# Moving tiles of the pairs made two words longer and read from the third word on, in a float32r attention and squared-ReLU kernel

## The chip, the cores and the metric

One core of one Trainium2 chip runs the whole program in one launch. The metric is the device time of a run in microseconds (us). The kernel before was run three times: the median is 1607.09 us, the lowest 1606.95, the highest 1607.5.

## What is computed

Two stages. First, attention through 32 inducing points: the points attend to the 12480 tokens of each of 4 batches, then every token attends to the 32 results. Second, a wide layer with a squared ReLU, on all 49920 tokens. Cut to what matters:

```python
def mab(q, kv):
    s = scale * (q @ kv.transpose(0, 2, 1))
    s = s - s.max(-1, keepdims=True)
    a = np.exp(s)
    a /= a.sum(-1, keepdims=True) + 1e-09
    return a @ kv
h = mab(I, x)              # I: (4, 32, 128), x: (4, 12480, 128)
y = mab(x, h)              # (4, 12480, 128)
...
h = y @ w_in               # (49920, 128) @ (128, 2048)
r = np.maximum(h, 0.0)
g = s * (r * r) + b
out = g @ w_out            # (49920, 2048) @ (2048, 128)
```

## The kernel before

The tokens are cut into 104 blocks of 480 (26 for each batch). The attention weights of a block on the 32 points stand in a tile `a2t` of 128 x 480 words: 32 rows of rounded values (float32r) and 32 rows of what the rounding left, each twice. The 32 results times `w_in` are formed once for each batch and stand in `wst` (128 x 2048, float32r), in parts that match the rows of `a2t`. So one matmul with `wst` as weights (stationary) and `a2t` as the streamed operand (moving) gives 128 of the 2048 hidden values of 480 tokens. Sixteen such matmuls make a block; the function `pair` issues them two at a time (L834), 8 pairs for each block.

What follows a pair: a ReLU of the two results (`r`, L849 on ACT or L851 on DVE), a product ReLU(h)·r, which is the square in float32 (`g`, L870 on DVE), a square rounded to float32r (`g1`, L911 on ACT, for one pair or for two at a time), and the difference of the two, `g2` = `g` − `g1` (L888, on POOL for most pairs, on DVE for the rest). Then the second layer: `out_part` (L936) multiplies `g1` with `w_hi` and with `w_lo`, the rounded and the left-over part of `w_out`, and `g2` with `w_hi`: three matmuls of 128 x 128 weights and 480 moving columns for each 128 hidden values, all accumulated in one PSUM bank. So a pair needs 2 matmuls of L834 and 6 of L936, all float32r. Only the first five pairs are done another way (`NATIVE = 5`): their squares in plain float32 times `w_out` in float32. At the end of a block the sum is scaled (L944) and stored (L948). Between the pairs stand the attention of later blocks (`attend`) and the first attention of the next batch (`scores`, `top`, `values`, `points`).

The order of all this is set when the program is built, by a small planner (`Plan`): each piece of work names its engine, an assumed time and what it waits for, and the planner picks. It knows nothing of addresses.

`a2t` comes in a ring of 3 buffers, `g2` in 8, `g1` in 4 (of four 480-word rows each, for two pairs), `g` in 4, `r` in 2. Except for the first block, an `a2t` tile is filled by four DMAs from the tile `hl` (`spread`, L805, on SP's queue). In the first block it is made by four transposes with a float32r identity `identr` (L788, in `attend_first`) and a copy. `identr` is written once at the start (L216) and is used nowhere else. `accb` is a tile of the same size in the pool `sm`: the sums of `values`, used from the second batch's preparation on (L670, L672, L692).

In the built program each tile begins at a multiple of 32 bytes of its partition. The moving tiles `a2t`, `g1` and `g2`, and with them every 480-word row of them, begin at multiples of 64 bytes. Of the three `a2t` buffers one begins at a multiple of 256 bytes, the two others 128 bytes behind one; the rows of `g1` and `g2` begin 64 or 192 bytes behind one. The last tile of the memory ends 64 bytes below the end of the partition's 224 KiB.

Of the kernel before, what the change touches and what calls it, by code (L numbers as in the profile page):

```python
# [11 lines left out]
F32R = mybir.dt.float32r  # L12
# [7 lines left out]
P = 128  # L20
T = 120
NQ = 4
BLK = T * NQ
# [124 lines left out]
def tile_attn_relu2(ctx: ExitStack, tc: tile.TileContext, xT, xN, indT, w_in, w_out, s_rep, b_rep, outT):  # L148
# [12 lines left out]
    const = ctx.enter_context(tc.tile_pool(name="const", bufs=1))  # L161
# [3 lines left out]
    p2 = ctx.enter_context(tc.tile_pool(name="p2", bufs=2))  # L165
    wst_pool = ctx.enter_context(tc.tile_pool(name="wst", bufs=2))
    sm = ctx.enter_context(tc.tile_pool(name="sm", bufs=2))
    ew = ctx.enter_context(tc.tile_pool(name="ew", bufs=1))
# [29 lines left out]
    def ring_in_order(name, bufs):  # L198

        n, free = ring(name, bufs)  # L200
        if n == 0:
            plan.events[name, "got", -1] = 0.0
        return n, (free, (name, "got", n - 1))
# [8 lines left out]
    bias = const.tile([P, 1], F32, name="bias")  # L212
    ident = const.tile([P, P], F32, name="ident")
    make_identity(nc, ident)
    identr = const.tile([P, P], F32R, name="identr")
    nc.vector.tensor_copy(out=identr, in_=ident)  # L216
    ones = const.tile([P, M], F32, name="ones")
    nc.vector.memset(ones, 1.0)
# [21 lines left out]
    def landing(us):  # L240

        dma[0] = max(dma[0], plan.end + 3.0) + us
        return dma[0]
# [458 lines left out]
    a2t, halves = {}, {}  # L702

    def attend(b, g, ps, *waits):
# [42 lines left out]
        for q in mine:  # L747
            plan.spawn(spread(b, g, q), SPREAD, plan.end + LAT)

    def attend_first(ps):  # L750
# [36 lines left out]
            w = A[:, q].rearrange("p r s i -> p (r s i)")  # L787
            nc.tensor.transpose(ps[:, q * T:(q + 1) * T].bitcast(F32R), w, identr[0:T, 0:T])  # L788
        yield dict(ACT=0.57, DVE=0.66), 0.0, *free
        t = p2.tile([P, BLK], F32R, name="a2t", bufs=3)  # L790
        plan.set(("a2t", "got", n))
        copy(t, ps[:, 0:BLK])
        a2t[0, 0] = t, n
# [3 lines left out]
    def spread(b, g, q):  # L797

        turn, free = ring_in_order("a2t", 3)
        yield "SP", 2.4, *free, ("hl", b, g)  # L800
        t = p2.tile([P, BLK], F32R, name="a2t", bufs=3)
        plan.set(("a2t", "got", turn))
        hl, n, left = halves[b, g]
        for r in range(P // M):
            nc.sync.dma_start(  # L805
                out=t[M * r:M * (r + 1)].bitcast(F32), in_=hl[M * q:M * (q + 1), r % 2].bitcast(F32)
            )
        left.remove(q)
        if not left:
            plan.set(("hl", n))  # L810
        a2t[b, GR * g + q] = t, turn
        plan.events["a2t", b, GR * g + q] = landing(0.7)
# [10 lines left out]
    def pair(k):  # L823
# [18 lines left out]
        q = quad[k - n]  # L842
# [40 lines left out]
        n2, free2 = ring("g2", 8)  # L883
        yield ("Pool", 2.237, ("Q", k), free2) if kind == "P" else ("DVE", 1.065, C_U, ("Q", k), free2)
        hi = q["g1_t"][:, half, :]
        g2 = ew.tile([P, 2, BLK], F32R, name="g2", bufs=8)
        eng = nc.gpsimd if kind == "P" else nc.vector
        eng.tensor_tensor(out=g2, in0=g, in1=hi.bitcast(F32), op=ALU.subtract)  # L888
        plan.set(("h", turn) if kind == "D" else ("g", g_turn))
# [9 lines left out]
    def square(k0):  # L899

        q = quad[k0]
        yield "ACT", 0.893, *([] if "g1_t" in q else [q["g1"][1]])
        done = [n for n, us in q["R"] if us + LAT <= plan.start + 0.01]
        lo, hi = done[0], done[-1] + 1
        del q["R"][:len(done)]
        if hi - lo == 2:
            plan.extend(0.8)
        if "g1_t" not in q:
            q["g1_t"] = ew.tile([P, 4, BLK], F32R, name="g1", bufs=4)
        sl = slice(2 * lo, 2 * hi)  # L910
        nc.scalar.activation(out=q["g1_t"][:, sl, :], in_=q["r_t"][:, sl, :], func=AF.Square)  # L911
        for i in range(lo, hi):
            plan.set(("Q", k0 + i))
            pr = (k0 + i) % NPAIR
            ops = [(w[:, 2 * pr + u, :], q["g1_t"][:, 2 * i + u, :]) for u in range(2) for w in (w_lo, w_hi)]
            plan.spawn(
                out_part(k0 + i, ops, 4 * MM, "w_split", lambda: g1_used(q)), k0 + i + OUT_HI, plan.end + LAT
            )
        if q["R"]:
            plan.spawn(square(k0), k0 + 1 + SQ, q["R"][0][1] + LAT)  # L920
        q["r_uses"] -= hi - lo
        if q["r_uses"] == 0:
            plan.set(("r", q["r"][0]))
# [191 lines left out]
```

## Time and profile before

| | |
|---|---|
| median of 3 runs | 1607.09 us (1606.95 to 1607.5) |
| the profiled execution: first to last instruction | 1605.5 us |
| granted TensorE clock, mean | 0.998 |
| matmul records | 8183 |
| of these float32r, 480 columns: L834 and L936 with w_hi, w_lo | 1664 + 3308 + 1654 = 6626 |
| DMA moved | 130.19 MB, mean 81 GB/s |

The page gives the profiled execution's span; of its own time around the span it shows nothing. PE, PEld, DVE, ACT, POOL and SP are the engines. [...] In grouped rows stand the count behind an x, the busy time, and the mean of one in ns; in rows in order of time the start, the length from the first start to the last end in us, and the count.

### The profile page before, as it was taken

The page shows a single profiled execution, that of the slowest core. Times are in us where ns is not written, and L with a number is a line of the kernel's source. Part 1 is how long each engine was busy: PE and PEld are TensorE (multiplying, and loading weights), DVE is VectorE, ACT ScalarE, POOL GpSimd, SP SyncE. Part 2 cuts the span into 40 slices and gives each one's busy share as a digit, 9 for nine tenths or more (in the row PEclk, how much of TensorE's full clock was granted, in tenths as well). Part 3 has the DMA queues.
Part 4 walks back from the last instruction along what each step waited for, and adds up shares of the span by engine and source line. Part 5 has one row for each costly group of instructions (what it writes and reads, how often), then busy time and mean ns, then how long its engine had stood idle before and what let it go on. Part 6 is the DMA issues. An engine that isn't in the chain of part 4 may idle for free.

```text
span 1605.5 us, 24656 instructions
## 1 busy us (share of the span) xinstructions
PE 1590.8 (99%) x8183; PEld 1294.8 (81%) x8183; DVE 1493.6 (93%) x1610; ACT 1476.7 (92%) x1694; POOL 1499.9 (93%) x677
## 2 busy tenths in 40 slices
PE   9899999999999999999999999999999999999998
PEld 6577888888887788888788787888888888888887
DVE  5999999999999999999999899999899999999997
ACT  7799989999999999999999998999999999999997
POOL 0299999999999999999999999999999999999998
PEclk9999999999999999999999999999999999999999
DMA  7332224212133233221213322321222112112100
GB/s 266 100 106 94 79 87 148 62 50 88 42 101 118 76 116 116 73 71 56 79 59 99 100 85 99 117 81 62 72 64 65 37 50 68 32 50 68 56 29 22
DMA packets 53981, 130.19 MB, mean 81 GB/s; under 512 B 11488, under 2 KB 37984, under 8 KB 53856
## 3 DMA queue, kind: packets, MB, share of 16 engines
q1 hardware_dynamic: 53856, 128.63, 25.0%
q8 instruction: 66, 1.08, 0.3%
q14 instruction: 59, 0.48, 0.1%
HBM read 73.52 MB, written 25.56 MB: 62 GB/s over the span
## 4 chain that ended last, share of the span: by engine, by line
PE 97%; DVE 1%; DMA 0%; ACT 0%; issue 0%; SPq 0%; ACTq 0%
PE x L936 67%; PE h L834 24%; PE x L712 2%; PE x L660 1%; PE x L615 1%; PE h L409 1%; DMA xt<-in_xT_dram 0%; PE x L463 0%; DVE g L870 0%; PE h L463 0%; PE x L565 0%; PE x L434 0%; PE h L434 0%; DVE wst L313 0%; DVE g L308 0%
## 5 line engine op out<-in xcount | busy, mean ns | idle before, releaser
L888 POOL TENSOR_TENSOR g<-g,g 128x960 fp32r<-128x960 f32 x670 | 1498.8, 2287 | 98.9 <-DVE g L870 79.6
L936 PE MATMUL x<-g,w_hi 128*128 128x480 f32 x3308 | 1074.3, 380 | 0.0
L911 ACT ACTIVATE g<-r 128x960 fp32r<-128x960 f32 (+1 forms) x761 | 803.2, 1079 | 34.0 <-DVE r L851 13.4
L870 DVE SCALAR_TENSOR_TENSOR g<-h,r 128x960 f32<-128x960 f32 x675 | 761.4, 1147 | 29.9 <-ACT r L849 20.5
L936 PEld LDWEIGHTS x<-g,w_hi 128*128 128x128 f32 x3308 | 621.1, 188 | 101.5 <-issue 3.1
L849 ACT ACTIVATE r<-h 128x960 f32<-128x960 f32 x638 | 612.1, 969 | 59.7 <-PE h L834 48.4
L936 PE MATMUL x<-g,w_lo 128*128 128x480 f32 x1654 | 628.7, 380 | 0.0
L834 PE MATMUL h<-a2t,wst 128*128 128x480 f32 x1664 | 511.7, 389 | 6.3 <-DVE g L870 4.6
L834 PEld LDWEIGHTS h<-a2t,wst 128*128 128x128 f32 x1664 | 300.0, 188 | 107.8 <-issue 38.8
L936 PEld LDWEIGHTS x<-g,w_lo 128*128 128x128 f32 x1654 | 310.3, 188 | 52.9 <-issue 3.1
L851 DVE TENSOR_SCALAR r<-h 128x960 f32<-128x960 f32 x194 | 223.7, 1153 | 25.3 <-PE h L834 18.8
L870 DVE SCALAR_TENSOR_TENSOR h<-h,r 128x960 f32<-128x960 f32 x157 | 181.5, 1157 | 7.9 <-ACT r L849 7.3
L888 DVE TENSOR_TENSOR g<-h,g 128x960 fp32r<-128x960 f32 x157 | 180.2, 1149 | 5.6 <-ACT g L911 0.8
L944 ACT ACTIVATE ob<-x,bias,s_sb 128x480 f32<-128x480 f32 x104 | 78.2, 752 | 14.3 <-PE x L936 14.0
L712 PE MATMUL x<-xt,hT 128*32 128x480 f32 x208 | 28.3, 578 | 0.0
L743 DVE TENSOR_TENSOR hl<-x,hl 128x480 fp32r<-128x480 f32 (+1 forms) x28 | 18.4, 656 | 10.1 <-ACT hl L179 10.1
L615 PE MATMUL x<-xt,ind_sb 128*32 128x480 f32 x156 | 21.2, 578 | 0.0
L718 DVE STREAM_TRANSPOSE x<-x 128x480 f32<-128x480 f32 (+1 forms) x28 | 19.2, 687 | 1.6 <-PE x L712 1.6
L660 PEld LDWEIGHTS x<-xn,eT 128*32 128x32 f32 (+1 forms) x630 | 17.5, 109 | 4.0 <-issue 2.7
L660 PE MATMUL x<-xn,eT 128*32 128x128 f32 (+1 forms) x630 | 20.7, 274 | 0.0
L736 DVE STREAM_TRANSPOSE x<-x 128x480 f32<-128x480 f32 (+1 forms) x28 | 19.5, 697 | 1.0
L734 DVE TENSOR_TENSOR x<-x,l 128x480 f32<-128x480 f32 (+1 forms) x28 | 18.6, 665 | 1.0
(147 smaller groups left out, 367.0 us busy)
## 6 DMA issues: line engine op xcount, KB each, us to landing
xt<-in_xT_dram SPq DMA_DIRECT2D x41, 960.0 KB, 5.3
out_dram<-ob SPq DMA_DIRECT2D x104, 240.0 KB, 2.0
a2t<-hl SPq DMA_DIRECT2D x412, 60.0 KB, 2.0
xn<-in_xN_dram SPq DMA_DIRECT2D x18, 512.0 KB, 5.1
xn<-in_xN_dram SPq DMA_DIRECT2D x18, 448.0 KB, 5.7
xt<-in_xT_dram SPq DMA_DIRECT2D x13, 480.0 KB, 4.2
wst<-hl SPq DMA_DIRECT2D x64, 64.0 KB, 2.0
r<-in_xT_dram SPq DMA_DIRECT2D x7, 480.0 KB, 9.5
```

Of the source, the lines that this page charges most:

```text
L615: nc.tensor.matmul(ps[M * q:M * (q + 1), 0:BLK], ind_sb, xt[:, q], start=True, stop=True)
L660: nc.tensor.matmul(ps[M * c:M * (c + 1), 0:P], eT[0:rows, n], xn_tiles[b, g, half][0][0:rows, n - half * TH], start=m < P // M, stop=m + P ...
L712: nc.tensor.matmul(ps[M * q:M * (q + 1), 0:BLK], hT[:, 0:M], xt[:, q], start=True, stop=True)
L736: nc.vector.transpose(out=s, in_=s)
L834: nc.tensor.matmul(h[:, u, 0:BLK], wst[:, c * P:(c + 1) * P], A, start=True, stop=True)
L849: nc.scalar.activation(out=r, in_=hv, func=AF.Relu)
L851: nc.vector.tensor_scalar(out=r, in0=hv, scalar1=0.0, scalar2=None, op0=ALU.max)
L870: nc.vector.scalar_tensor_tensor(out=g, in0=hv, scalar=0.0, in1=r, op0=ALU.max, op1=ALU.mult)
L888: eng.tensor_tensor(out=g2, in0=g, in1=hi.bitcast(F32), op=ALU.subtract)
L911: nc.scalar.activation(out=q["g1_t"][:, sl, :], in_=q["r_t"][:, sl, :], func=AF.Square)
L936: nc.tensor.matmul(o, w, g, start=first and n == 0, stop=left == 0 and n == len(ops) - 1)
L944: nc.scalar.activation(out=ob, in_=o, func=AF.Identity, bias=bias, scale=s_sb)
```

## The change

The tiles `a2t`, `g1` and `g2` get two words (8 bytes) more in each partition, and the program uses them from the third word on: the copy, the DMAs, the squares and the differences write there, and the matmuls read there. Nothing else of their shape changes. `identr` gives up its own tile and becomes the first user of the tile `accb`, which exists anyway (`bufs=1`).

```diff
-    identr = const.tile([P, P], F32R, name="identr")
+    identr = sm.tile([P, P], F32R, name="accb", bufs=1)
     nc.vector.tensor_copy(out=identr, in_=ident)
...
-        t = p2.tile([P, BLK], F32R, name="a2t", bufs=3)
+        t = p2.tile([P, BLK + 2], F32R, name="a2t", bufs=3)[:, 2:]
...
-        g2 = ew.tile([P, 2, BLK], F32R, name="g2", bufs=8)
+        g2 = ew.tile([P, 2 * BLK + 2], F32R, name="g2", bufs=8)[:, 2:].rearrange("p (u t) -> p u t", u=2)
...
-            q["g1_t"] = ew.tile([P, 4, BLK], F32R, name="g1", bufs=4)
+            q["g1_t"] = ew.tile([P, 4 * BLK + 2], F32R, name="g1", bufs=4)[:, 2:].rearrange("p (u t) -> p u t", u=4)
```

(The line of `a2t` stands twice, in `attend_first` and in `spread`.) In the built program a tile of 1928 bytes takes 1952, one of 3848 takes 3872 and one of 7688 takes 7712, so every moving row now begins 8 bytes behind a multiple of 32 bytes, and the buffers of one ring no longer stand alike against multiples of 64, 128 or 256 bytes. All tiles behind `ident` move: by 512 bytes down, and from the first `a2t` on by less. `wst`, the weights of L834, began at a multiple of 64 bytes and now begins 32 behind one; `w_hi` and `w_lo` stay where they were.

No instruction is added, removed or moved on any engine, and no wait. All that the order of PE shows is the new name of the identity in the four transposes of the first block (`x` is the PSUM tile that they write, `h` and `g` with L1052 are matmuls whose results nobody reads):

```order
 L1052 MATMUL h<-g_113 128x448 x4
 L1052 MATMUL h<-g_113 128x384
-L788 MATMUL x_85<-identr,hl 128x120 x4
+L788 MATMUL x_85<-accb,hl 128x120 x4
 L1052 MATMUL h<-g_113 128x384 x2
 L712 MATMUL x_86<-xt,hT 32x480 x4
```

The same four instructions stand at the same place. On DVE the cast that writes the identity (L216) has the new name, too; ACT, POOL and SP are the same row for row.

More of the change, by code (lines that the diff above doesn't have):

```diff
@@ L800, in spread @@
         yield "SP", 2.4, *free, ("hl", b, g)
-        t = p2.tile([P, BLK], F32R, name="a2t", bufs=3)
+        t = p2.tile([P, BLK + 2], F32R, name="a2t", bufs=3)[:, 2:]
         plan.set(("a2t", "got", turn))
```

## The prediction

> **What bounds the kernel now.** I read the page from the top: busy shares, the chain that ended last, then the stages.
>
> ```profile
> span 1605.5 us, 24656 instructions
> PE 1590.8 (99%) x8183; PEld 1294.8 (81%) x8183; DVE 1493.6 (93%) x1610; ACT 1476.7 (92%) x1694; POOL 1499.9 (93%) x677
> PE 97%; DVE 1%; DMA 0%; ACT 0%; issue 0%; SPq 0%; ACTq 0%
> PE x L936 67%; PE h L834 24%; PE x L712 2%; PE x L660 1%; PE x L615 1%; PE h L409 1%; DMA xt<-in_xT_dram 0%; PE x L463 0%; DVE g L870 0%; PE h L463 0%; PE x L565 0%; PE x L434 0%; PE h L434 0%; DVE wst L313 0%; DVE g L308 0%
> ```
>
> The chain is PE for 97% of the span, and 91% are the two lines whose moving tiles the change touches. So a nanosecond more or less in each of these matmuls is on the path from the first to the last. How many there are, and what the others cost, the groups say:
>
> ```profile
> L888 POOL TENSOR_TENSOR g<-g,g 128x960 fp32r<-128x960 f32 x670 | 1498.8, 2287 | 98.9 <-DVE g L870 79.6
> L936 PE MATMUL x<-g,w_hi 128*128 128x480 f32 x3308 | 1074.3, 380 | 0.0
> L911 ACT ACTIVATE g<-r 128x960 fp32r<-128x960 f32 (+1 forms) x761 | 803.2, 1079 | 34.0 <-DVE r L851 13.4
> L936 PE MATMUL x<-g,w_lo 128*128 128x480 f32 x1654 | 628.7, 380 | 0.0
> L834 PE MATMUL h<-a2t,wst 128*128 128x480 f32 x1664 | 511.7, 389 | 6.3 <-DVE g L870 4.6
> ```
>
> 3308 + 1654 + 1664 = 6626 float32r matmuls of 480 columns. One of them on average 1 ns faster or slower is 6.6 us, 0.41% of the span.
>
> The busy time by stages (first the stretch and its length, then PE, PEld, DVE, ACT, POOL with counts, clock, DMA share, GB/s):
>
> ```profile
> 105.00:400.00 295.00, 294.92 (x1553) 240.12 (x1552) 277.01 (x290) 272.23 (x313) 289.19 (x130) 1.00 0.28 90
> 400.00:700.00 300.00, 300.00 (x1556) 244.75 (x1555) 282.13 (x301) 279.35 (x317) 293.87 (x132) 1.00 0.27 89
> 700.00:1000.00 300.00, 299.94 (x1430) 242.96 (x1429) 281.84 (x294) 278.06 (x310) 295.38 (x133) 1.00 0.27 84
> 1000.00:1300.00 300.00, 299.82 (x1561) 248.96 (x1561) 281.55 (x299) 282.72 (x329) 293.43 (x133) 1.00 0.23 72
> 1300.00:1560.00 260.00, 260.00 (x1199) 217.15 (x1198) 249.26 (x253) 248.21 (x273) 253.71 (x114) 1.00 0.15 46
> ```
>
> PE has no idle time in these 1455 us, but POOL has little: 289.19 + 293.87 + 295.38 + 293.43 + 253.71 = 1425.6 busy, 29.4 idle. DVE has 83 us, ACT 94. The order and the share of each engine stay as they are, so however fast PE gets, POOL lets this part shrink by 29 us at most. That caps any gain: 1605.5 − 29.4 = 1576.
>
> **What one of these matmuls costs, and whether the place of its moving tile matters.** Lines of one window (duration min/median/max, first and last start), a row in order of time of the plain float32 matmuls at the start, and a piece of the chain:
>
> ```profile
> L936 PE MATMUL x<-g,w_hi x56: 373/381/385, 72.1 to 99.8; 128*128 128x480 f32 x56
> L936 PE MATMUL x<-g,wst x16: 564/566/566, 62.2 to 69.5; 128*128 128x480 f32 x16
> 64.20 1.77 PE L936 MATMUL x<-g,wst 128*128 128x480 f32 x4
> 1593.47 7.83 PE x L936 x36
> ```
>
> The pace of float32r is 7.83/36 = 217.5 ns for 480 columns. Plain float32 takes two records for one product; four of them span 1.77 us, less the last one's 0.566 that is 1.204/3 = 401 ns each, and all 16 lie within 2 ns. If float32r streamed at exactly twice that pace it would need 201 ns. It needs 16 to 17 ns more, and its records scatter over 12 ns (373 to 385) where the slow ones don't. So something in the fast stream stumbles, for some 17 ns × 6626 = 110 us in all, and not always alike.
>
> The Trainium skill, "TensorE: Matmul & The Clock Gate", section "Single matmul latency", gives (398 + N)/2.4 ns for a warm matmul: 366 for 480 columns, and 566 for 960, as two cycles for each column would be. The slow rows agree with it to the nanosecond, the float32r median of 381 is 15 above it; by the page, too, there would be some 100 us to gain.
>
> Does the place of the tile count? The three `a2t` buffers take turns, block after block, and stand differently against 256 bytes. Three blocks in turn (the middle one has the buffer at a multiple of 256), and two stretches of four matmuls each:
>
> ```profile
> L834 PE MATMUL h<-a2t,wst x16: 379/382/383, 1321.1 to 1335.3; 128*128 128x480 f32 x16
> ...
> L834 PE MATMUL h<-a2t,wst x16: 375/377/456, 1337.7 to 1348.9; 128*128 128x480 f32 x16
> ...
> L834 PE MATMUL h<-a2t,wst x16: 374/382/455, 1350.9 to 1363.0; 128*128 128x480 f32 x16
> ...
> 1334.16 0.60 PE L834 MATMUL h<-a2t,wst 128*128 128x480 f32 x2
> 1334.60 0.60 PE L936 MATMUL x<-g,w_hi 128*128 128x480 f32 x2
> 1335.04 0.60 PE L834 MATMUL h<-a2t,wst 128*128 128x480 f32 x2
> ...
> 1344.78 0.59 PE L834 MATMUL h<-a2t,wst 128*128 128x480 f32 x2
> 1345.20 0.59 PE L936 MATMUL x<-g,w_hi 128*128 128x480 f32 x2
> 1345.63 0.59 PE L834 MATMUL h<-a2t,wst 128*128 128x480 f32 x2
> ```
>
> In the first and third block the median is 382, in the middle one 377. Four matmuls in a row, two of each line, take 1335.04 − 1334.16 = 0.88 us in the first and 1345.63 − 1344.78 = 0.85 in the middle block: 220 and 212.5 ns each (to about 2.5, as the starts are rounded to 10 ns). The kinds of instructions are the same, the start of `a2t` is another. So the start does matter, by some 7 ns at this place. What no row shows is a start that is not a multiple of 64 bytes.
>
> **The change part by part.**
>
> *The matmuls (6626).* Instructions, columns and order stay. The price is the shift of the start, and rows of this trace bound it from both sides. Best: all go like the middle block, 212.5 for 217.5, −5 ns × 6626 = −33 us, of which POOL lets through 29. Worst of what the rows show: all like the first block, 220, +2.5 ns × 6626 = +17 us. I take −2 ns, −13 us: less than half of the best case, because only the ends of a stream of 480 words see the shift, and because some of what PE gains will be spent on waiting for POOL, whose steady idle share is 2%. It leans to the faster side since the stream has 17 ns to lose against 2.5 to the slow row, not since any row shows this start.
>
> *The weights.* `wst` now starts 32 bytes behind a multiple of 64. Its loads (188 ns, below) lie under matmuls that start 217 ns apart, so 30 ns more would stay hidden; beyond that each ns costs 1.7 us.
>
> ```profile
> L834 PEld LDWEIGHTS h<-a2t,wst 128*128 128x128 f32 x1664 | 300.0, 188 | 107.8 <-issue 38.8
> ```
>
> *POOL, DVE and ACT on shifted tiles.* They read and write the same 960 words from another start. I take nothing. If the shift cost POOL one more access in 240, that is 2287/240 = 9.5 ns × 670 = 6.4 us, within its 29 us. It sets the end only from 29.4 us/670 = 44 ns (1.9%) for each operation. ACT and DVE have more cover.
>
> *The a2t DMAs.* 412 of 60 KB, now landing 8 bytes off:
>
> ```profile
> L805 SPq DMA_DIRECT2D a2t<-hl x412: 507/582/2295, 57.8 to 1564.8; - x138
>   DMA wst<-hl: 1.4, 1
> DMA to landing us min/median/max: 1.9/2.0/5.5
> ```
>
> They land in 2.0 us; the only DMA that matmuls of L834 ever waited for is that of `wst`, once, 1.4 us. The ring of three tiles lets them run a block ahead (1605.5/104 = 15.4 us), so even a doubling is hidden. Without that cover it would be 2 us × 103 blocks.
>
> *The identity.* Written once, read by four matmuls until 47 us; `accb` is first written at 241.0:
>
> ```profile
> L788 PE MATMUL x<-identr,hl x4: 245/249/278, 46.5 to 46.8; 120*128 120x120 f32 x4
> L670 DVE COPY accb<-x x3: 292/292/293, 241.0 to 1020.1; 128x128 f32<-128x128 f32 x3
> ```
>
> 194 us lie between, so sharing costs no wait.
>
> Sum: 1605.5 − 13 = 1592.5 for the profiled execution. The median of the runs is 1.6 us above its span, carried over: 1594.
>
> **The rivals.**
>
> *Nothing happens.* The stumbling belongs to the fast stream itself, or to steps of 64 bytes and more; the old starts (0, 64, 128, 192 against 256) are then merely replaced by a spread that averages the same. For it: the fast and the slow `a2t` blocks already mix in the 217.5, and the new starts are spread over all places. Against it: the mean would have to stay within 0.5 ns, where places differ by 7. Time 1607.
>
> The Trainium skill, "SBUF — State Buffer", section "Specifications (TRN2)", gives 16-byte cachelines and asks for two hits in each for full bandwidth. By that rule, a start at the third word still finds two words in the first line and in the last, so it costs nothing and brings nothing. The trace agrees only in part: with four words in each line, the stream is 17 ns short of double pace already.
>
> *Slower: one more group for each stream.* If the words are fetched in groups of at least four, a start in the middle of one cuts the first and the last: 121 groups instead of 120. The stream is at its limit (it already runs below double pace), so nothing hides it: 217.5/120 = 1.8 ns × 6626 = +12 us, from the first block on, 1619. With groups of 16 words it would be 31 for 30, 7.2 ns, 48 us, 1655. It decides as soon as the fetch, not the array, sets the pace, which the 16 ns speak for. Against it: the half groups of one stream's end and the next one's start may be fetched side by side, and the blocks whose `a2t` starts 128 bytes on show that a stream can be slower with no group cut.
>
> *Faster than forecast.* If the shift removes the stumbling altogether, PE needs 201 instead of 217 and POOL sets the end: 1578.
>
> **How the numbers follow.** Faster 0.43: 1594 as the likeliest, 1577 to 1603 as its range. Nothing 0.25: 1604 to 1610. Slower 0.32: of it 0.22 around 1619 (to 1624, the row at 220 for all), 0.10 beyond, towards 1655. The range from 1577 to 1624 leaves out these 0.10 and some 0.05 below. 0.2%, 3.2 us, is about what a measurement of this kernel can tell from no change; it is 0.5 ns for each matmul.
>
> **What would show it.** In the profile of the changed kernel: a chain piece of 36 matmuls of L936 at 7.76 us or less (7.83 now) says faster, 7.89 or more the extra group. The float32r records' minimum, median and maximum (373/381/385) should move down and draw together if the stumbling goes. POOL's idle time in the five stretches should fall from 29 to about 16 us at 1594, and PE should begin to show idle time. POOL's mean should stay at 2287 ns and the DMAs of `a2t` at 2.0 us. I am wrong if PE's pace doesn't move, if it moves up, or if another engine's mean changes by more than its cover.

## The result, and the profile after

The changed kernel takes 1616.36 us (median of 4 runs, 1616.22 to 1616.57), the kernel before on the same chip 1607.30 (1606.95 to 1607.77): a ratio of 1.0056 (95% interval 1.0042 to 1.007), so 9.1 us slower. The range of the prediction holds that time, but its likeliest case, 1594, had the wrong sign.

The page of the kernel after: span, busy shares, and the chain that ended last by engine and by line.

```profile
span 1614.5 us, 24656 instructions
PE 1600.5 (99%) x8183; PEld 1305.1 (81%) x8183; DVE 1493.9 (93%) x1610; ACT 1479.3 (92%) x1694; POOL 1254.2 (78%) x677
PE 97%; DVE 2%; issue 0%; DMA 0%; ACT 0%; DVEq 0%
PE x L936 68%; PE h L834 23%; PE x L712 2%; PE x L660 1%; PE x L615 1%; PE h L409 1%; DVE g L870 0%; PE x L434 0%; PE x L463 0%; DMA xt<-in_xT_dram 0%; PE h L463 0%; PE x L565 0%; PE h L434 0%; DVE w_lo L323 0%; DVE wst L313 0%
```

Counts and chain are those of before: still PE for 97%, still the same two lines for 91%. PE's busy time grew by 9.7 us. What fell is POOL, from 1499.9 to 1254.2 us. The groups (busy, mean ns of one, idle before):

```profile
L888 POOL TENSOR_TENSOR g<-g,g 128x960 fp32r<-128x960 f32 x670 | 1253.0, 1894 | 352.2 <-ACT g L911 170.8
L936 PE MATMUL x<-g,w_hi 128*128 128x480 f32 x3308 | 1081.1, 382 | 0.0
L911 ACT ACTIVATE g<-r 128x960 fp32r<-128x960 f32 (+1 forms) x761 | 804.5, 1080 | 34.6 <-DVE r L851 11.7
L936 PE MATMUL x<-g,w_lo 128*128 128x480 f32 x1654 | 633.0, 383 | 0.0
L834 PE MATMUL h<-a2t,wst 128*128 128x480 f32 x1664 | 510.9, 388 | 5.9 <-DVE g L870 4.3
L834 PEld LDWEIGHTS h<-a2t,wst 128*128 128x128 f32 x1664 | 302.5, 189 | 106.0 <-issue 34.3
```

One subtraction on POOL takes 1894 ns in place of 2287, the same 670 of them. ACT's squares (1079, now 1080) and the weight loads (188, now 189) are what they were. The matmuls of L936 are 2 to 3 ns longer. The stages, the same stretches as before:

```profile
105.00:400.00 295.00, 295.00 (x1546) 240.59 (x1545) 275.67 (x288) 271.07 (x310) 242.00 (x130) 1.00 0.29 90
400.00:700.00 300.00, 300.00 (x1547) 245.20 (x1546) 280.42 (x300) 277.92 (x316) 243.87 (x132) 1.00 0.28 88
700.00:1000.00 300.00, 300.00 (x1418) 244.24 (x1417) 280.03 (x291) 277.81 (x312) 244.82 (x132) 1.00 0.27 84
1000.00:1300.00 300.00, 299.93 (x1558) 248.86 (x1557) 280.23 (x299) 280.38 (x324) 243.58 (x131) 1.00 0.23 69
1300.00:1560.00 260.00, 260.00 (x1191) 217.27 (x1190) 248.37 (x249) 247.11 (x272) 212.47 (x114) 1.00 0.16 50
```

PE has no idle time, as before, but gets through fewer matmuls (x1546 for x1553, 1547 for 1556, 1418 for 1430, 1191 for 1199). The fifth column of busy time is POOL's: 1186.7 of 1455 us for 1425.6 before, 268 us idle for 29. The clock is 1.00 in all five, and the mean spacing from the start of one such matmul to the next (read as below) goes from 217.5 to 217.8 ns up to 219.1 to 219.5 in each of them. So the loss runs through all stages alike; that is a change of pace. Rows of one window (min/median/max), and the last piece of the chain:

```profile
L936 PE MATMUL x<-g,w_hi x58: 374/382/389, 71.8 to 100.0; 128*128 128x480 f32 x58
...
L936 PE MATMUL x<-g,wst x16: 563/566/566, 62.0 to 69.4; 128*128 128x480 f32 x16
```

```profile
1602.31 7.95 PE x L936 x36
```

The float32r records scatter over 15 ns in place of 12, the plain float32 ones stand at 566 as before, and 36 matmuls of L936 take 7.95 us, 220.8 ns each, for 217.5.

**Where the 9 us are.** In PE's order there are 6543 places where one of the 6626 float32r matmuls directly follows another. I read the spacing from start to start at each, since a record (382 ns) is longer than the way to the next start. Spacings of at most 232 ns (all but 206 of the 6543 before, all but 237 after) have a mean that I call the pace; what longer spacings have over the pace, I call waiting. The rest of PE's time is then what other matmuls take. Before: pace 217.60 ns, waiting 23.4 us, rest 152.3. After: 219.28, 21.1, 152.5. So the pace costs 1.68 × 6543 = 11.0 us, the waiting is 2.3 us less, the rest adds 0.2: 8.9 us, and the spans differ by 9.0. In all sixteen kernels of the table below the rest lies between 151.6 and 153.8 us, so the table's pace and waiting account for the times. One execution of e7, of 4523.68 us, is left out of its ratio; no cause is on record.

### The profile page after: what moved, and what is told of

The parts are those of the page before. It is cut to its first block, busy times and chain, and to the rows that moved or that the text cites. A ratio compares the mean times of both kernels' runs of the same rounds, so it can differ in the third digit from the quotient of the medians.

```text
span 1614.5 us, 24656 instructions
## 1 busy us (share of the span) xinstructions
PE 1600.5 (99%) x8183; PEld 1305.1 (81%) x8183; DVE 1493.9 (93%) x1610; ACT 1479.3 (92%) x1694; POOL 1254.2 (78%) x677
## 4 chain that ended last, share of the span: by engine, by line
PE 97%; DVE 2%; issue 0%; DMA 0%; ACT 0%; DVEq 0%
PE x L936 68%; PE h L834 23%; PE x L712 2%; PE x L660 1%; PE x L615 1%; PE h L409 1%; DVE g L870 0%; PE x L434 0%; PE x L463 0%; DMA xt<-in_xT_dram 0%; PE h L463 0%; PE x L565 0%; PE h L434 0%; DVE w_lo L323 0%; DVE wst L313 0%
## 5 line engine op out<-in xcount | busy, mean ns | idle before, releaser
L888 POOL TENSOR_TENSOR g<-g,g 128x960 fp32r<-128x960 f32 x670 | 1253.0, 1894 | 352.2 <-ACT g L911 170.8
L936 PE MATMUL x<-g,w_hi 128*128 128x480 f32 x3308 | 1081.1, 382 | 0.0
L911 ACT ACTIVATE g<-r 128x960 fp32r<-128x960 f32 (+1 forms) x761 | 804.5, 1080 | 34.6 <-DVE r L851 11.7
L870 DVE SCALAR_TENSOR_TENSOR g<-h,r 128x960 f32<-128x960 f32 x675 | 761.7, 1148 | 31.6 <-ACT r L849 23.4
L936 PEld LDWEIGHTS x<-g,w_hi 128*128 128x128 f32 x3308 | 625.4, 189 | 101.7 <-issue 2.4
L936 PE MATMUL x<-g,w_lo 128*128 128x480 f32 x1654 | 633.0, 383 | 0.0
L834 PE MATMUL h<-a2t,wst 128*128 128x480 f32 x1664 | 510.9, 388 | 5.9 <-DVE g L870 4.3
L834 PEld LDWEIGHTS h<-a2t,wst 128*128 128x128 f32 x1664 | 302.5, 189 | 106.0 <-issue 34.3
L936 PEld LDWEIGHTS x<-g,w_lo 128*128 128x128 f32 x1654 | 313.3, 189 | 53.4 <-issue 3.1
L888 DVE TENSOR_TENSOR g<-h,g 128x960 fp32r<-128x960 f32 x157 | 180.4, 1150 | 5.3 <-ACT g L911 0.4
L743 DVE TENSOR_TENSOR hl<-x,hl 128x480 fp32r<-128x480 f32 (+1 forms) x28 | 18.4, 656 | 10.6 <-ACT hl L179 10.6
```

Of the source, the lines that this page charges most:

```text
L834: nc.tensor.matmul(h[:, u, 0:BLK], wst[:, c * P:(c + 1) * P], A, start=True, stop=True)
L870: nc.vector.scalar_tensor_tensor(out=g, in0=hv, scalar=0.0, in1=r, op0=ALU.max, op1=ALU.mult)
L936: nc.tensor.matmul(o, w, g, start=first and n == 0, stop=left == 0 and n == len(ops) - 1)
```

## The experiments

Most of them change only where the streamed tiles start. The first word is the word of the tile at which the used part begins; tiles start at multiples of 32 bytes. The column POOL is the mean of L888 in ns; ratios are to the kernel before on the same chip.

| run | first words, other edits | median us | ratio (95%) | pace ns | waiting us | POOL |
|---|---|---|---|---|---|---|
| before | 0 | 1607.3 | | 217.60 | 23.4 | 2287 |
| after | 2 | 1616.36 | 1.0056 (1.0042 to 1.007) | 219.28 | 21.1 | 1894 |
| e1 | 0, tiles longer | 1608.41 | 1.0005 (0.9996 to 1.0014) | 217.83 | 23.1 | 2297 |
| e2 | e1, a2t 2 | 1609.15 | 1.0009 (1.0 to 1.0018) | 217.99 | 22.6 | 2298 |
| e3 | e1, g2 2 | 1610.52 | 1.0017 (1.0008 to 1.0026) | 218.14 | 22.7 | 2281 |
| e4 | e1, g1 2 | 1611.09 | 1.002 (1.0011 to 1.0029) | 218.28 | 22.6 | 1895 |
| e5 | 4 | 1605.74 | 0.999 (0.9981 to 0.9998) | 217.21 | 24.7 | 2282 |
| e6 | 1 | 1628.77 | 1.0132 (1.0118 to 1.0146) | 221.89 | 16.3 | 1890 |
| e7 | 0, g 2 | 1607.67 | 1.0003 (0.9994 to 1.0013) | 217.62 | 23.1 | 1892 |
| e8 | 0, a2t at 256 bytes | 1604.91 | 0.9985 (0.9976 to 0.9993) | 216.94 | 24.6 | 2279 |
| e9 | 3 | 1598.9 | 0.9948 (0.9933 to 0.9963) | 215.88 | 26.2 | 2290 |
| e10 | e8, pool `ew` 64 bytes lower | 1608.18 | 1.0005 (0.9996 to 1.0014) | 217.80 | 22.4 | 2286 |
| e11 | e7, planner told of POOL | 1601.61 | 0.9964 (0.9952 to 0.9977) | 217.55 | 18.0 | 1895 |
| e12 | e11 and a2t at 256 bytes | 1601.05 | 0.9962 (0.995 to 0.9975) | 217.40 | 18.8 | 1897 |
| e13 | all 8 bytes past 256 | 1614.14 | 1.0037 (1.0024 to 1.005) | 218.74 | 21.5 | 1892 |
| e14 | all at 256 | 1603.72 | 0.9975 (0.9965 to 0.9985) | 216.80 | 25.2 | 2292 |
| e15 | e13, planner told of POOL | 1609.38 | 1.001 (1.0 to 1.002) | 219.06 | 17.2 | 1894 |
| e16 | all 12 bytes past 256, g 2, planner told of POOL | 1589.22 | 0.9884 (0.9867 to 0.99) | 215.21 | 21.1 | 1897 |

### Is it the third word, or that tiles grew and moved?

Tiles as long as the change makes them, in the same places, but used from word 0; then one of the three used from word 2.

```diff
-        t = p2.tile([P, BLK + 2], F32R, name="a2t", bufs=3)[:, 2:]
+        t = p2.tile([P, BLK + 8], F32R, name="a2t", bufs=3)[:, 0:0 + BLK]
```

(and alike for `g2` and `g1`; `0:0 + BLK` is `2:2 + BLK` where a run uses word 2.)

> All tiles stand exactly where the change put them, but a2t, g1 and g2 are used from their first word. Theory 'cut group' (a stream that starts in the middle of a 16-byte group pays for one more): PE's pace goes back from 219.1 to about 217.6 ns, time about 1606 to 1608. Theory 'placement' (the new starts against 64, 128 and 256 bytes cost the 9 us): pace stays near 219, time 1614 to 1617. For POOL, 'two words' says that L888 goes back from 1894 to about 2287 ns; 'placement' says it stays near 1894.

> Same placement, only a2t from the third word on. 'Cut group': the 1664 matmuls of L834 alone pay some 1.4 ns each, +2.3 us on e1. 'Placement': as e1. POOL touches no a2t, so L888 is as in e1 by either theory.

> Same placement, only g2 from the third word on. 'Cut group': the 1654 matmuls with g2 pay, +2.3 us on e1. 'Placement': as e1. For POOL this shifts the output against both inputs: if the output's place against the inputs is what counts, L888 goes to about 1894 ns here and not in e4; if it is the second input against the first, it stays as in e1.

> Same placement, only g1 from the third word on. 'Cut group': the 3308 matmuls with g1 pay, +4.6 us on e1. 'Placement': as e1. For POOL this shifts the second input against the first: if that is what counts, L888 goes to about 1894 ns here and not in e3.

Growth, the moved tiles and the shared identity together cost 0.7 us (1608.41 for 1607.69 of the kernel before on the same chip), within what a measurement can tell from none. So the first word costs some 8 of the 9 us (1616.36 − 1608.41 = 7.95). One tile at a time it costs 0.74, 2.11 and 2.68 us over e1 (by the intervals of the ratios each is good to some 1.4 us, so the first is not told from nothing); the sum is 5.5, and 2.4 more come only when all three are shifted. The paces say the same: 0.16, 0.31 and 0.45 ns for one tile each, 1.45 for all. That is no fixed fee for each matmul: `a2t` and `g2` have nearly the same number (1664 and 1654) and pay 0.7 and 2.1. With `g2` alone shifted (e3), the spacing from a `g2` matmul to the next `g2` matmul stays (217.85, now 217.8 ns), and that from `g2` to `a2t` grows from 217.60 to 219.46. So it counts which stream follows which.

e4 shows more: POOL is fast again (1895 ns) as soon as `g1` is shifted and `g` is not. POOL's inputs are `g` and `g1`.

### Other first words

> Placement of the changed kernel, all three moving tiles used from the fifth word on (16 bytes). 'Cut group' with groups of 16 bytes: no group is cut, so PE's pace is that of e1, 217.8 ns, time about 1608, and L888 on POOL is back near 2290 ns if POOL's gain is two input streams that must not start at the same place of a 16-byte group. If the group is 32 bytes or more, the pace stays at 219 or above, time about 1615 to 1617, and L888 may stay at 1894.

> Same placement, all used from the second word on (4 bytes). 'Cut group' of four words: one group more for each stream as with two words, pace 219.3, time about 1616. If words are fetched in pairs, an odd start cuts every pair and the streams become much slower (over 1650). L888: if POOL fetches pairs, a shift of one word leaves the two inputs in the same pair: near 2290; if any shift within 16 bytes does, near 1894.

> Placement of the changed kernel, all three moving tiles used from the fourth word on (12 bytes). Theory 'pairs and groups' (words come in pairs of 8 bytes inside groups of 16; a start that cuts a group costs some 1.5 ns for each matmul, one that cuts the pairs some 4): as from the second word, pace near 221.9, time 1627 to 1630. Theory 'the later in the group the dearer': above 1630. L888 on POOL near 1890 by both.

Word 4 is near word 0 (1605.74, 2.7 us below e1; its rows also stand 16 bytes further against 256). Word 1 costs 20 us over e1 and lies between the two times that I had expected (1616, or over 1650), word 2 costs 8, word 3 gains 9.5 (1598.9). All three cut a group of four words at both ends, so a fee for cut groups is refuted: it would charge word 3 as much as word 1. My expectation for word 3, a fee for a cut group and a larger one for a cut pair of words, missed by 28 us and more; and POOL, expected near 1890 ns, took 2290.

### POOL's subtraction

`g`, which no matmul reads, two words longer and used from the third; the other tiles stand against 256 bytes as in the kernel before (the identity is in `accb`, and a spare tile keeps the places).

```diff
-        g = hv if kind == "D" else ew.tile([P, 2, BLK], F32, name="g", bufs=4)
+        g = hv if kind == "D" else ew.tile([P, 2 * BLK + 2], F32, name="g", bufs=4)[:, 2:].rearrange("p (u t) -> p u t", u=2)
```

> The kernel before, with identr in accb and a spare tile of 256 bytes in its place, so that all else moves by 256 bytes and keeps its place against them; and only g, the first input of POOL's L888, which no fast matmul streams, is two words longer and used from the third. If L888 depends on the two inputs' starts against each other, it falls to about 1894 ns as in e4, and PE's pace stays at 217.6: time 1604 to 1608, since PE sets the end. If it is g1's own start that counts, L888 stays at 2287.

Page of e7:

```profile
span 1605.5 us, 24657 instructions
PE 1591.5 (99%) x8183; PEld 1295.6 (81%) x8183; DVE 1492.8 (93%) x1611; ACT 1476.3 (92%) x1694; POOL 1252.4 (78%) x677
L888 POOL TENSOR_TENSOR g<-g,g 128x960 fp32r<-128x960 f32 x670 | 1251.3, 1892 | 345.2 <-ACT g L911 153.8
```

POOL has the whole gain, 247 us, and the time is the same to 0.03%: nothing that sets the end waited for POOL. For the gain to be of use, the planner has to know of it. Its price for a subtraction on POOL stands in the code; I set it to what is measured, and POOL then does 786 of the differences and DVE 41 (670 and 157 before):

```diff
-            pool_work[0] = max(pool_work[0], plan.end) + 2.237
+            pool_work[0] = max(pool_work[0], plan.end) + 1.85
...
-        yield ("Pool", 2.237, ("Q", k), free2) if kind == "P" else ("DVE", 1.065, C_U, ("Q", k), free2)
+        yield ("Pool", 1.85, ("Q", k), free2) if kind == "P" else ("DVE", 1.065, C_U, ("Q", k), free2)
```

> e7 (g from the third word, POOL's L888 at 1892 ns) with the planner told 1.85 us for a POOL difference instead of 2.237. It then gives POOL 790 of the 827 differences instead of 670. Theory 'PE alone sets the end': the freed time of DVE and ACT buys nothing, 1605 to 1609. Theory 'the late vectors cost PE some of its idle 15 us': 1600 to 1604.

Page of e11:

```profile
span 1599.8 us, 24783 instructions
PE 1586.3 (99%) x8183; PEld 1297.8 (81%) x8183; DVE 1455.2 (91%) x1568; ACT 1408.3 (88%) x1538; POOL 1459.9 (91%) x793
```

1601.61 us. The pace is that of before (217.55); the gain is in the waiting, 23.1 to 18.0 us. DVE and ACT have 38 and 68 us less to do, which fits; but the planner also orders PE's matmuls otherwise here, and which of the two brings the gain was not tried.

### The place against 256 bytes

In e8 `a2t` has tiles of 512 words, so that all three start at a multiple of 256 bytes. In e10 the pool of `g1`, `g2`, `r` and `g` also lies 64 bytes lower. e12 joins e8's `a2t` to e11.

```diff
-        t = p2.tile([P, BLK], F32R, name="a2t", bufs=3)
+        t = p2.tile([P, 512], F32R, name="a2t", bufs=3)[:, 0:BLK]
```

> The kernel before, with identr in accb; the freed 512 bytes go into a spare tile of 128 and into a2t tiles of 512 words, so that all three a2t buffers start at a multiple of 256 bytes and everything from ob on stands where it stood. Theory 'the place against 256 bytes counts' (from the blocks of the kernel before: 216.8 ns on average where a2t stands at 0, 218.0 where it stands at 128): two blocks in three gain 1.2 ns for each of 64 matmuls, about -5 us, 1602. Theory 'only groups of 16 bytes count': no change, 1607.

> e8 with wj and lw in one buffer each (64 bytes less), so that g2, r, g1 and g stand 64 bytes lower: the rows of g2 and g1 now start at 128 and 0 against 256 bytes instead of 192 and 64. If a start at 0 is fast and one at 128 slow for these tiles as for a2t, their pace stays where it is on average, 217 ns, time 1603 to 1607. If the whole effect of the place is how a stream's end meets the next one's start, the pace moves by up to 1 ns either way: 1598 or 1612.

> What helped, together: a2t at multiples of 256 bytes (tiles of 512 words used from word 32), g from the third word, the planner told 1.85 us for POOL; wj, lw and mrow in one buffer each and a spare tile of 64 bytes keep g2, r and g1 at their old places against 256 bytes. If the gains add: e8's -2.4 us and whatever e11 brings, 1600 to 1605. If the new order eats it, above 1607.

`a2t` at 256 bytes gains 2.4 us (interval of the ratio below 1) where 5 were expected: the pace gives 0.66 × 6543 = 4.3 us, and 1.2 of it turn into waiting. In this kernel the blocks at 256 are thus the faster ones, as the prediction read. But moving the others by 64 bytes, from rows 64 and 192 past 256 to rows 0 and 128 past, takes 3.3 us back. In e12 the two gains do not add: 1601.05 for 1601.61, inside the intervals, and the pace (217.40) is not that of e8 (216.94), although the waiting is near that of e11. One thing more differs: in the built programs `wst`, the weights of L834, begins at a multiple of 256 bytes in the kernel before, e8, e10 and e11, but 128 bytes past one in e12 (what the weights' place does is measured below). The place of one tile has no price of its own.

### One stretch by itself

This kernel leaves the whole computation out: stretches of 96 back-to-back float32r matmuls from two tiles in turn, one line for each start, weights at a multiple of 256 bytes, and then subtractions on POOL, six for each choice of starts.

```python
for i in range(N): mm(out[i % 2][:, 0:480], W[:, i % 2, :], T[i % 2][:, 2:482], start=True, stop=True)
for i in range(6): tt(out=C[:, 0:0 + 960], in0=A[:, 0:0 + 960], in1=B[:, 2:2 + 960], op=ALU.subtract)
```

> Leaves the whole computation out and stores zeros: 35 stretches of 96 float32r matmuls, back to back with two weights in turn, each stretch on a line of its own with another first word (0 to 64), length (476 to 484) or order of its moving tiles, and beside the first of them 18 stretches of six POOL differences with other first words of the two inputs and the output. Theory 'start': the first word's place in the 16-byte group sets the cost, 1 > 2 > 0 > 3, some 222, 219, 217.5, 216 ns, whatever the last word is: stretches with first word 2 and 478, 480 or 482 columns then differ by 0.42 ns per column alone. Theory 'end': the last group counts: first word 0 with 482 columns is as dear as first word 2 with 480 (some +2 ns beyond the two columns), and first word 2 with 478 or 482 columns, which ends on a group, is as cheap as first word 0. Theory 'meeting': contiguous rows (0 and 480 of one tile) are cheaper than two tiles with the same first word. Period of 16 bytes: words 4, 5, 6, 7 as 0, 1, 2, 3; of 32: not. POOL: if only the difference of the two inputs' first words counts, 1 and 2 (and 5 and 6) take about 1890 ns, 0, 3, 4, 8 and 16 about 2290, and the output's first word changes nothing.

In order of time, the first row of each stretch: L46 streams from word 0, L47 from 1, L48 from 2, L49 from 3, L50 from 4. The difference of two starts, divided by 96, is the pace.

```profile
30.97 0.38 PE L46 MATMUL o<-X,W 128*128 128x480 f32 x1
...
51.77 0.38 PE L47 MATMUL o<-X,W 128*128 128x480 f32 x1
...
72.89 0.38 PE L48 MATMUL o<-X,W 128*128 128x480 f32 x1
...
93.39 0.38 PE L49 MATMUL o<-X,W 128*128 128x480 f32 x1
...
113.87 0.38 PE L50 MATMUL o<-X,W 128*128 128x480 f32 x1
```

20.80, 21.12, 20.50 and 20.48 us: 216.7, 220.0, 213.5 and 213.3 ns from words 0, 1, 2 and 3. With nothing else running, word 2 is faster than word 0 by 3.2 ns, and in the kernel it is slower. Words 4 to 7 repeat 0 to 3 (216.7, 220.0, 213.4, 213.3). But the place against 256 bytes enters too: streams 32, 64 and 128 bytes past take 220.0, 218.3 and 213.4 ns, so 128 is faster here than 0, the other way round than in the kernel's `a2t` blocks. And so does the second stream's place. With both rows in one tile, 480 words apart, words 0 to 3 take 215.0, 221.6, 220.0 and 216.7 ns: word 2, 3.2 ns ahead of word 0 before, is 5 ns behind it. Its stretch is L73, and L74 is the next one:

```profile
593.43 0.38 PE L73 MATMUL o<-X,W 128*128 128x480 f32 x1
...
614.55 0.38 PE L74 MATMUL o<-X,W 128*128 128x480 f32 x1
```

Nor does the pace grow evenly with the length: from word 0, 476 and 478 columns take 213.3 to 213.4 ns, 480 take 216.7, 482 take 220.0, 484 take 218.7. None of the three theories of the expectation holds: the order of the words is 1, 0, 2, 3; 482 columns from word 0 are dearer than 480 from word 2; and rows in one tile are cheaper from word 0 alone.

POOL's groups: L80 has both inputs from word 0, in L81 to L83 the second one starts at word 1, 2 and 3.

```profile
L83 POOL TENSOR_TENSOR C<-A,B 128x960 fp32r<-128x960 f32 x6 | 13.6, 2258 | 0.5
...
L80 POOL TENSOR_TENSOR C<-A,B 128x960 fp32r<-128x960 f32 x6 | 13.5, 2254 | 9.9 <-DVEq L118 9.5
...
L82 POOL TENSOR_TENSOR C<-A,B 128x960 fp32r<-128x960 f32 x6 | 11.3, 1888 | 0.5
...
L81 POOL TENSOR_TENSOR C<-A,B 128x960 fp32r<-128x960 f32 x6 | 11.3, 1887 | 0.5
```

One or two words apart (against groups of four): 1888 ns. None or three: 2256. Both inputs from word 2 are slow again (2268), and the start of the output changes nothing, as expected. So it is how the two inputs stand to each other, which the change altered by shifting `g1` and not `g`.

### All streams alike

Rows 480 words apart stand at ever other places against 256 bytes. Here every row lies 512 words behind the last, and every stream starts at one place.

```diff
-        g2 = ew.tile([P, 2 * BLK + 8], F32R, name="g2", bufs=8)[:, 0:0 + 2 * BLK].rearrange("p (u t) -> p u t", u=2)
+        g2 = ew.tile([P, 2, 512], F32R, name="g2", bufs=8)[:, :, 18:18 + BLK]
```

(and alike for `a2t` and `g1`, against e1; the tiles begin 192 bytes past 256, so `18` is 8 bytes past and `16`, in e14, none. For the room, three small tiles have one buffer and `e` shares the tiles of `ob`.)

> The diff's first cost is two words more for each moving tile; here every row that TensorE streams instead lies on a pitch of 512 words, and every stream, of the identity's tiles, of the pairs and of the differences alike, starts 8 bytes past a multiple of 256 (e shares ob's tiles, and three small tiles have one buffer, for the room). Theory 'meeting': the shift cost time because rows 480 words apart and tiles two words longer start at ever other places against 256 bytes, so that one stream's pace is set by how it meets the next; where all start alike the kernel has the pace of the isolated stretch from word 2, 213.3 to 213.5 ns, which is 4.1 to 4.3 ns below the kernel before times 6626, about -28 us: 1578 to 1585, less the part that the other engines then bound. Rival 'cut group': a stream that starts inside a group of four words costs a group more, whatever its neighbours: 219 ns and 1614 to 1618. POOL's subtractions: 1890 ns, since the inputs' first words differ by two (g from word 0, g1 from word 2).

> The kernel of the pitch of 512 words, but every stream starts at a multiple of 256 bytes. Theory 'meeting': the pace of the isolated stretch from word 0, 216.7 ns, 0.9 ns below the kernel before: about -6 us, 1600 to 1603. Rival 'cut group': no group is cut, as in the kernel before, so 1605 to 1608, and 10 us faster than the kernel that starts 8 bytes past; by the theory it is 15 to 25 us slower than that one. POOL's subtractions: 2280 to 2300 ns, since both inputs start at a multiple of 16 bytes.

> The kernel with every stream 8 bytes past a multiple of 256, with the planner told 1.85 us for a subtraction on POOL in place of 2.237 (one number in two places), so that POOL takes more of the differences from VectorE. If TensorE still sets the end there, the same time within 0.2 per cent; if the vector engines bind once TensorE needs 28 us less, 3 to 10 us faster than it, 1572 to 1580. By the rival 'cut group' TensorE is slower than before, POOL's gain is worth nothing, and the time is that of the kernel without the number, 1614 to 1618.

Half of it came true. At 256 the kernel has the pace of the isolated stretch (216.80 for 216.7) and 1603.72 us (1600 to 1603 expected). Eight bytes past, it has 218.74 for 213.5, and 1614.14 us in place of the 1578 to 1585 expected. So the loss stays where all neighbours are alike. As an account of the kernel the theory fell, although in the isolated stretches, with weights at 256, unlike rows do slow word 2. That e14 is 10 us faster than e13 is what the cut group would give, which e9 had refuted. e15 gains 4.8 us over e13 in the median, and as in e11 it is the waiting that fell (21.5 to 17.2 us), where the rival 'cut group' had expected no gain.

Two things pointed on. In e13, 1249 of the 1650 spacings from a `w_lo` matmul to the next `w_hi` matmul are 220 ns, most of the others 213 or 214. And a least-squares fit of e13's spacings on the share of each in which POOL, DVE or ACT worked gives POOL −0.03 ns (standard error 0.10) and no group of DVE's or ACT's instructions more than 0.8 either way, where 5 ns were to be explained: no sign that the other engines slow them. What differed from the isolated stretch was where the weights lie: at a multiple of 256 there, 64 bytes past (`w_hi`, `w_lo`) and 192 past (`wst`) here.

### The weights' place

The isolated stretches again, now with weights and streams both moved; the computation is left out.

```python
for i in range(N): mm(out[i % 2][:, 0:480], W[:, i % 2, (16, 16)[i % 2]:(16, 16)[i % 2] + 128], T[i % 2][:, 2:2 + 480], start=True, stop=True)
```

> Leaves the whole computation out: back-to-back float32r matmuls of 480 columns only, 96 to a stretch and line, streams from word 0, 1, 2 or 3 (two tiles at multiples of 256 bytes in turn) crossed with weights that start 0, 16, 32, 48, 64, 96, 128, 160, 192 or 224 bytes past a multiple of 256 (both weights alike, or two starts in turn). In the kernel whose streams all start 8 bytes past a multiple of 256, the pairs' matmuls repeat at 220 ns in most records and at 213 in the rest, w_hi and w_lo start 64 bytes past 256 and wst 192 past; the isolated stretches at 213.3 ns had weights at a multiple of 256. Theory 'weights': the pace hangs on where the weights stand against the stream, since both are read at a time (weight loads are busy 81 per cent of the span beside the matmuls): from word 2, weights at 0 give 213.3 ns and weights at 64 give 219 to 220; from word 0, weights at 64 give 215 to 217. Rival 'other engines or the wait': the weights' place changes no pace by more than 0.5 ns (216.7, 220.0, 213.3 and 213.3 ns from words 0 to 3 for every place), and what takes the isolated pace away in the kernel is the other engines or the waits.

First rows of the stretches with weights 64 bytes past 256 (L56 to L59: words 0 to 3; L60 is the next one) and 192 past (L72 to L75, then L76):

```profile
363.66 0.38 PE L56 MATMUL o<-X,W 128*128 128x480 f32 x1
...
384.39 0.38 PE L57 MATMUL o<-X,W 128*128 128x480 f32 x1
...
405.53 0.38 PE L58 MATMUL o<-X,W 128*128 128x480 f32 x1
...
426.64 0.38 PE L59 MATMUL o<-X,W 128*128 128x480 f32 x1
...
447.13 0.39 PE L60 MATMUL o<-X,W 128*128 128x480 f32 x1
...
698.68 0.38 PE L72 MATMUL o<-X,W 128*128 128x480 f32 x1
...
719.64 0.38 PE L73 MATMUL o<-X,W 128*128 128x480 f32 x1
...
740.75 0.38 PE L74 MATMUL o<-X,W 128*128 128x480 f32 x1
...
761.87 0.38 PE L75 MATMUL o<-X,W 128*128 128x480 f32 x1
...
782.35 0.38 PE L76 MATMUL o<-X,W 128*128 128x480 f32 x1
```

L58 to L59 is 21.11 us: from word 2, weights 64 bytes past, 219.9 ns. L59 to L60 is 20.49: word 3, same weights, 213.4. All ten places in this way, in ns (good to 0.1, as the starts are rounded to 10 ns):

| weights past 256, bytes | word 0 | word 1 | word 2 | word 3 |
|---|---|---|---|---|
| 0 | 216.7 | 220.0 | 213.5 | 213.3 |
| 16 | 220.0 | 220.0 | 216.8 | 213.4 |
| 32 | 220.0 | 220.0 | 213.3 | 213.3 |
| 48 | 215.5 | 220.2 | 213.4 | 213.3 |
| 64 | 216.0 | 220.1 | 219.9 | 213.4 |
| 96 | 217.9 | 221.3 | 219.9 | 213.4 |
| 128 | 217.8 | 223.2 | 220.0 | 213.4 |
| 160 | 220.0 | 220.0 | 216.8 | 216.6 |
| 192 | 218.3 | 220.0 | 219.9 | 213.3 |
| 224 | 220.0 | 223.3 | 220.0 | 213.4 |

The theory's numbers came out: the weights' place moves word 2 from 213.5 to 219.9 and leaves word 3 alone. The rival, no change above 0.5 ns, is refuted. Weighted by the kernel's matmuls (4962 with weights 64 past, 1664 with 192), words 0, 2 and 3 give 216.6, 219.9 and 213.4; the kernels with all streams alike have 216.80 (e14), 218.74 (e13) and, below, 215.21 (e16). The first fits, the other two are 1.2 and 1.8 ns off, and no run here says why. In the kernels with unlike rows, `w_hi` and `w_lo` begin 64 bytes past 256 and `wst` 96. The order of these kernels over the first words (e9 215.88, e1 217.83, after 219.28, e6 221.89) is that of the rows 64 and 96 of the table too: 3, 0, 2, 1. Only the order: by these rows word 2 would cost 3.4 ns over word 0, and it costs 1.45; no isolated stretch has rows and weights placed as in these kernels.

It isn't the whole rule. Where the two weights of a stretch lie 512 bytes further apart, word 2 with weights 64 past is back at 213.4; where weights 64 and 192 past take turns, word 3 is at 216.7 and word 2 at 218.3.

### A kernel from word 3

Every stream 12 bytes past 256, with e11's planner and a `g` shifted by two words, so that POOL's inputs lie one word apart.

```diff
-        g2 = ew.tile([P, 2, 512], F32R, name="g2", bufs=8)[:, :, 18:18 + BLK]
+        g2 = ew.tile([P, 2, 512], F32R, name="g2", bufs=8)[:, :, 19:19 + BLK]
```

> The kernel with every row on a pitch of 512 words and the planner's 1.85 us for POOL, but every stream starts 12 bytes past a multiple of 256 in place of 8 (word 3 in place of 2); g is two words longer and used from its third word, so that POOL's two inputs differ by one word; t4 shares the small tile of mrows, for the room. Theory 'weights': from word 3 the isolated pace is 213.3 ns with weights 64 and with weights 192 bytes past 256, where they stand in the kernel, and 216.6 where the two take turns, as they do where a2t's matmuls meet the pairs'; so 213.5 to 214.5 ns here, 3.1 to 4.1 ns below the kernel before, times 6626: 20 to 27 us, 1580 to 1587; if VectorE and ScalarE (busy 1456 and 1411 us in the kernel from word 2) bind first, up to 1592. POOL's subtraction 1890 ns. Rival 'the kernel adds its own 5 ns' (what the stream from word 2 lost between the isolated stretch and the kernel comes from waits or other engines): 217 to 219 ns and 1603 to 1612.

Page and groups of e16, and the last piece of its chain:

```profile
span 1587.1 us, 24783 instructions
PE 1573.5 (99%) x8183; PEld 1297.4 (82%) x8183; DVE 1452.4 (92%) x1568; ACT 1406.2 (89%) x1538; POOL 1459.3 (92%) x793
...
L888 POOL TENSOR_TENSOR g<-g,g 128x960 fp32r<-128x960 f32 x786 | 1458.1, 1897 | 121.3 <-DVE g L870 82.3
L936 PE MATMUL x<-g,w_hi 128*128 128x480 f32 x3308 | 1086.7, 378 | 0.0
```

```profile
1573.10 10.25 PE x L936 x48
```

1589.22 us, 1.16% below the kernel before and 1.7% below the change: the best of all. The chain is still PE for 97%. The last 48 matmuls of L936 run at 213.5 ns (10.25/48), the isolated pace. The mean is 215.21, above the 213.5 to 214.5 expected and below the rival's 217, and the time is 2 us above the 1580 to 1587 expected: the spacing from a `w_hi` matmul to the next `w_lo` matmul is 217.2 on average, in about half the cases 219, while `w_lo` to `w_hi` runs at 214.2. Why these two differ was not tried. Against the kernel before, the pace gives 2.39 × 6543 = 15.6 us and the waiting 2.3: 17.9 of the 18.4 us between the spans.

## Why the prediction was wrong

- **What bounds the kernel: right.** PE for 97%, 6626 matmuls, about 6.6 us for each ns. The runs obey it: pace and waiting of PE alone explain every time in the table.
- **The stumbling and the place of the tile: right as an observation.** All isolated paces of 480 columns lie between 213.3 and 223.3 ns where the weights start at a multiple of 16 bytes, and by e8 the a2t blocks at 256 are the faster ones in this kernel. That is no rule for the place: alone, with weights at 256, a stream 128 bytes past is faster than one at 256 (213.4 and 216.7 ns). The formula that the prediction set beside its records, from the Trainium skill, "TensorE: Matmul & The Clock Gate", "Single matmul latency", is given there for a single bf16 matmul; no run here shows that float32r could reach it.
- **The matmul term, −2 ns × 6626 = −13 us: the step that failed.** It measured +1.68 ns, +11.0 us. The bounds (−5 and +2.5) held it; the choice between them was made by "it leans to the faster side since the stream has 17 ns to lose". Room to gain is no evidence of direction. Besides, the step asked only where the stream starts. What stands around it decides with it: from the same word 2 a stretch takes 213.5 ns, but 219.9 with the weights 64 bytes past 256, where `w_hi` and `w_lo` stood and stay, and 220.0 with weights at 256 and its two rows 480 words apart. That the first word costs the 8 us is shown by e1; how the single paces add up to its 1.45 ns is not, and neither is what makes them inside the chip.
- **POOL "I take nothing", and "should stay at 2287": wrong.** It went to 1894, 17% down. I looked for a dearer access and forgot that two inputs can move against each other. It bought next to nothing, for the reason the prediction gave: POOL is off the path. With POOL alone made faster, in e7, the waiting is 23.1 us for 23.4. Most of the 2.3 us less after the change thus go with the slower pace (at 221.89 ns the waiting is 16.3 us, at 215.88 it is 26.2). But with it fell the cap of 29 us, and so the floor of the range at 1577: POOL would no longer have bound there.
- **Weights, a2t's DMAs, the identity, ACT and DVE at nothing: right in size.** Weight loads 188 to 189 ns, the DMAs landing in 2.0 us as before, ACT 1080 for 1079 ns, and e1, which has the moved `wst` and the identity, within 0.05%. For the weights the prediction asked only how long a load takes, though; their place enters by the pace of the streams (from word 0 it is 216.7 ns with weights at 256 and 217.9 with weights 96 past, where the change put `wst`).

```profile
DMA to landing us min/median/max: 1.9/2.0/7.1
```

- **The rival "one more group": the sign and nearly the size (1619 for 1616.36), not the mechanism.** Its sign in the profile, a chain piece of 7.89 us or more, appeared (7.95), and still word 3, which cuts as many groups, is the fastest start. An agreeing number from one kernel did not show the cause; it took another start.
- **The rule on lines of 16 bytes.** The Trainium skill, "SBUF — State Buffer", "Specifications (TRN2)", asks for two hits in a line for full bandwidth: by that, words 0 and 2 should run alike, and words 1 and 3, with a single word in the first or last line, could pay. The same row puts a penalty on each cross to a new line, which words 1, 2 and 3 would pay alike. TensorE's streams here do neither: words 0 to 3 take 216.7, 220.0, 213.5 and 213.3 ns with weights at 256.

## What to carry to other kernels

When TensorE is busy all the time with float32r streams, measure the pace of a stretch by itself over the starts of the streams and of the weights together, with the rows as far apart as in the kernel, before choosing a layout: here the corners lay 10 ns (5%) apart, and neither address alone had a price. When a change speeds up an engine off the path, nothing happens until the plan gives it more work: the same 17% on POOL was worth nothing in e7 and 6 us in e11. And where rows bound a term from both sides, room on one side does not choose the sign.

## What the runs showed of the hardware that I had not expected

- A float32r matmul of 480 columns, back to back, often has a pace of 213.3, 216.7 or 220.0 ns (215.0 to 223.3 occur too), by the first word of the stream, its place and its neighbour's against 256 bytes, and the weights' place. With weights from word 1 and the stream from word 0 it is 233 ns. What does this inside the chip, no run shows.
- The pace from word 0 is 213.3 ns for 478 columns and 220.0 for 482: two columns more or less change it by more than their number.
- A subtraction of 960 words on POOL takes 1888 ns when its inputs start one or two words apart and 2256 when they start none or three apart.
